# Cutting the weight loads differently: W1's chunk 13 together with chunk 12, W2's chunks 9 to 12 in two slices

## The chip, the cores and the metric

The kernel runs on one core of a Trainium2 chip. The metric is the device time of one execution in microseconds (us); of several runs the median is given. Lower is better.

## What is computed

Linear attention over 8 batches, 8 heads, 576 positions and 64 channels, and then a two-layer network over the 4608 resulting rows of 512 channels:

```python
q_s = exp(q - max(q, -1)); q_s = q_s / sum(q_s, -1)      # per row
k_s = exp(k - max(k, 2));  k_s = k_s / sum(k_s, 2)       # over the positions
kv  = einsum('bhsd,bhse->bhde', k_s, v)                  # 64 x 64 per head
x   = einsum('bhsd,bhde->bhse', q_s, kv)                 # then heads side by side: (4608, 512)
h   = x @ w_in                                           # (4608, 2048)
g   = where(h > 0, h, exp(min(h, 0)) - 1)                # ELU
out = g @ w_out                                          # (4608, 512)
```

All inputs and the output are float32. W1 is `w_in` (512 x 2048, 4 MB), W2 is `w_out` (2048 x 512, 4 MB).

## The kernel before, in words

**Work and its order.** The hidden width of 2048 is cut into 16 chunks of 128 (`NCH`). A step (j, s) is chunk s of batch j; there are eight batches of 512 rows and a ninth group that collects the 64 rows left over from each batch. In `program` (L1146) each step runs, in this order: `hidden` (L882, with its matmuls in `hidden_mm`, L912), four matmuls 128x512 that make 128 hidden channels of 512 rows from X and W1; ScalarE's exponential (L895, or the pair L892 and L893 for some steps) and GpSimd's subtraction of one (L896); VectorE's combination into the tile GT (L925); and, three steps later (`LAG`), `project` (L927 to L936), four matmuls that add GT times the chunk's 128 rows of W2 to four output banks. So on TensorE a group of L912 and a group of L933 take turns, and the first projection needs W2's chunk 0 three steps after the first hidden product. A hidden product of chunk n writes one of three PSUM banks, the one that chunk n - 3 used; it waits until L925 has read that one.

**Queues.** The program is written out by hand as text tables. `START` (L42 to L50) is the order of the work on batch 0 before the steps begin; `FIRST` (L51 to L68) says what each step of batch 0 does besides its own work: three strings, the first run after the hidden matmuls, the second after the projection, the third after L925. The words of a string are carried out by `do` (L1018). Most of them belong to the attention of the next batch: `qmax`, `qsub`, `qexp`, `qsum`, `qmul` the softmax of Q; `kturn`, `kacross`, `diag`, `kspread`, `copy`, `ksub`, `kexp` the one of K; `vconv`, `kv`, `kfac` the product with V; `pturn` and `pturn0` (L744, L766) transposes by TensorE of the softmax of Q; `att`, `xc` the rows of X. `load` issues a load on SyncE's queue (SP), `hold` makes SP wait for the latest hidden product before it issues more.

**The weights.** `w1:a:b` loads W1's chunks a to b - 1 (`load_w1`, L252, issue at L255) and `w2:a:b` W2's (`load_w2`, L259, issue at L262). Both are issued by GpSimd (POOL) between its other instructions, into a queue of its own (q0 in the profile; SP's loads of Q, K and V are q1). One load has one semaphore: whoever needs any chunk of a slice waits until the whole slice has landed. A slice of W1 is 128 partitions times four row pieces of 512 bytes per chunk; a slice of W2 is 128 partitions times one row of 2048 bytes per chunk. The order of W loads before is, in `START`: W1 1-3, W1 0, W2 0-1, W1 4-5, W2 2, W1 6-8, W2 3, W2 4-5; in `FIRST`: step 1 W1 13, then W1 9-11; step 2 W2 6-8; step 4 W1 12, then W2 9-12; step 5 W1 14-15; step 12 W2 15, then W2 13-14. After batch 0 all weights stay in SBUF.

Of the kernel before, what the change touches and what calls it, by code (L numbers as in the profile page):

```python
# [15 lines left out]
R = 4  # L16
# [33 lines left out]
         "pwide:B:act w2:3:4 att:2 att:3 xc:2 load:Q:1:A load:Q:1:R w2:4:6 h:0:2 xc:3 kmax2:AB ")  # L50
FIRST = {  # L51
    0: ("qmax:A ksub:R:dve", "", "qsub:0:dve"),
    1: ("w1:13:14", "w1:9:12", "qsub:1:dve"),
    2: ("", "qmax0:R", "w2:6:9"),
    3: ("hold qexp:A", "load:Q:1:B:act", ""),
    4: ("w1:12:13", "w2:9:13", "load:K:1:R qsum:A qsub0:R:dve"),
    5: ("w1:14:16", "kturn", "kacross vconv:R qmax:C"),
    6: ("", "qmul:A hold", "load:V:1:RAB"),
    7: ("qexp0:R", "", "diag qsub:2:dve"),
# [1148 lines left out]
```

## Time and profile before

| | |
|---|---|
| median of 3 runs | 309.68 us |
| lowest and highest | 309.59 and 310.59 us |
| span of the profiled execution, first to last instruction | 308.1 us |
| median less that span | 1.6 us |
| TensorE busy | 297.6 us (97%) |
| VectorE, ScalarE, GpSimd busy | 235.0, 192.9, 171.3 us |
| moved by DMA | 51.63 MB, of it 8.39 MB on q0 |

The profile is of one execution. PE is TensorE's matmuls, PEld its loads of stationary operands, which overlap the matmuls; DVE is VectorE, ACT ScalarE, POOL GpSimd, SP SyncE. A row of the timeline has the start in us from the span's start, the time in us, the engine, the line, the operation with output and input, how many there are, and in brackets the idle time before it with what ended it. In a row of waits stand the total in us, how many times, and the longest. In a row of DMA issues stand how many, the size, and the time from issue to landing.

### The profile page before, as it was taken

The page shows a single profiled execution, that of the slowest core. Times are in us where ns is not written, and L with a number is a line of the kernel's source. Part 1 is how long each engine was busy: PE and PEld are TensorE (multiplying, and loading weights), DVE is VectorE, ACT ScalarE, POOL GpSimd, SP SyncE. Part 2 cuts the span into 40 slices and gives each one's busy share as a digit, 9 for nine tenths or more (in the row PEclk, how much of TensorE's full clock was granted, in tenths as well). Part 3 has the DMA queues.
Part 4 walks back from the last instruction along what each step waited for, and adds up shares of the span by engine and source line. Part 5 has one row for each costly group of instructions (what it writes and reads, how often), then busy time and mean ns, then how long its engine had stood idle before and what let it go on. Part 6 is the DMA issues. An engine that isn't in the chain of part 4 may idle for free.

```text
span 308.1 us, 4839 instructions
## 1 busy us (share of the span) xinstructions
PE 297.6 (97%) x1733; PEld 240.1 (78%) x1733; DVE 235.0 (76%) x400; ACT 192.9 (63%) x358; POOL 171.3 (56%) x215
## 2 busy tenths in 40 slices
PE   7789899999999999999999999999999999999995
PEld 4467677788878888888888888888888888888884
DVE  6988978979959897999889988998895353335442
ACT  2678975577559784877587758775877543334432
POOL 2968873686436743786278637863686333333440
PEclk9999999999999999999999999999999999999999
DMA  7999999985708993768475846590512030003004
GB/s 261 393 340 364 372 345 257 273 253 145 191 3 246 261 251 105 223 122 231 133 217 144 208 143 209 146 198 3 172 23 57 2 136 0 0 2 136 0 0 136
DMA packets 60584, 51.63 MB, mean 168 GB/s; under 512 B 26897, under 2 KB 50705, under 8 KB 60561
## 3 DMA queue, kind: packets, MB, share of 16 engines
q1 hardware_dynamic: 52960, 41.23, 47.7%
q0 software_dynamic: 6400, 8.39, 10.5%
q10 hardware_dynamic: 1200, 1.72, 2.0%
q8 instruction: 13, 0.21, 0.3%
q14 instruction: 11, 0.08, 0.1%
HBM read 38.27 MB, written 9.45 MB: 155 GB/s over the span
## 4 chain that ended last, share of the span: by engine, by line
PE 85%; DMA 6%; POOL 4%; ACT 2%; DVE 2%; issue 1%
PE bank L933 40%; PE bank L912 40%; DMA W2S<-in_moe_w_out_dram 5%; PE bank L827 2%; POOL W1S L255 1%; PE bank L598 1%; DMA QR<-in_q_dram 1%; POOL QR L679 1%; POOL QS L708 1%; PE bank L805 1%; DVE KT L326 1%; DVE QF L672 0%; PE bank L560 0%; ACT ES L895 0%; ACT ES L893 0%
## 5 line engine op out<-in xcount | busy, mean ns | idle before, releaser
L933 PE MATMUL bank<-W2S,GT 128*128 128x512 f32 x572 | 153.4, 391 | 1.4 <-DMA W2S<-in_moe_w_out_dram 1.2
L896 POOL TENSOR_SCALAR ES<-ES 128x512 f32<-128x512 f32 (+1 forms) x130 | 85.8, 662 | 117.3 <-ACT ES L895 117.3
L912 PE MATMUL bank<-XT,W1S 128*128 128x512 f32 x512 | 138.4, 392 | 0.5 <-issue 0.3
L925 DVE SCALAR_TENSOR_TENSOR GT<-bank,ES 128x512 fp32r<-128x512 f32 (+1 forms) x130 | 87.9, 681 | 54.4 <-PE bank L912 40.6
L933 PEld LDWEIGHTS bank<-W2S,GT 128*128 128x128 f32 x572 | 106.3, 188 | 23.6 <-DMA W2S<-in_moe_w_out_dram 1.6
L895 ACT ACTIVATE ES<-bank 128x512 f32<-128x512 f32 (+1 forms) x130 | 76.0, 592 | 70.9 <-PE bank L912 70.7
L912 PEld LDWEIGHTS bank<-XT,W1S 128*128 128x128 f32 x512 | 94.1, 188 | 19.9 <-ACT XT L814 0.9
L679 POOL TENSOR_TENSOR QR<-QR,QM 128x512 f32<-128x512 f32 (+1 forms) x21 | 24.9, 1187 | 0.6 <-DVE QM L672 0.5
L684 ACT ACTIVATE QR<-QR 128x1024 f32<-128x1024 f32 (+3 forms) x19 | 19.0, 1006 | 3.1 <-DVE QR L679 3.1
L855 ACT ACTIVATE XT<-bank 128x320 fp32r<-128x320 f32 (+1 forms) x30 | 15.0, 501 | 9.4 <-PE bank L827 9.3
L689 DVE TENSOR_REDUCE QZ<-QR 128x16 f32<-128x1024 f32 (+1 forms) x14 | 18.8, 1343 | 0.6 <-ACT QR L684 0.6
L672 DVE TENSOR_REDUCE QM<-QR 128x16 f32<-128x1024 f32 (+1 forms) x14 | 18.8, 1342 | 0.0
L912 PE MATMUL bank<-XTR,W1S 128*128 128x512 f32 x64 | 16.6, 389 | 0.0
L438 DVE TENSOR_TENSOR KR<-KR,NB 128x512 f32<-128x512 f32 x16 | 14.6, 938 | 0.0
L623 ACT ACTIVATE MB<-bank,KZ 64x64 fp32r<-64x64 f32 x44 | 10.1, 302 | 7.0 <-DVE KZ L614 6.9
L387 DVE TRANSPOSE_TENSOR_REDUCE KM<-KR 128x32 f32<-128x1024 f32 x12 | 14.4, 1226 | 0.0
L857 POOL CAST QT<-QW 128x1024 fp32r<-128x1024 f16 x12 | 12.5, 1039 | 2.9 <-DMA QW<-QS 2.9
L912 PEld LDWEIGHTS bank<-XTR,W1S 128*128 128x128 f32 x64 | 12.0, 188 | 2.5
L892 ACT ACTIVATE ES<-bank 128x512 f32<-128x512 f32 x15 | 8.9, 594 | 7.9 <-PE bank L912 7.9
L827 PE MATMUL bank<-QT,MB 128*128 128x320 f32 (+1 forms) x48 | 12.5, 300 | 0.7 <-ACT XT L855 0.7
L708 POOL TENSOR_TENSOR QS<-QR,QI 128x1024 f16<-128x1024 f32 (+1 forms) x7 | 12.5, 1783 | 0.4 <-DVE QI L691 0.4
L484 ACT ACTIVATE EK<-KR 128x1024 bf16<-128x1024 f32 x12 | 12.6, 1050 | 0.0
(108 smaller groups left out, 262.8 us busy)
## 6 DMA issues: line engine op xcount, KB each, us to landing
out_dram<-OSB SPq DMA_DIRECT2D x30, 256.0 KB, 2.7
KR<-in_k_dram SPq DMA_DIRECT2D x6, 1024.0 KB, 7.7
VR<-in_v_dram SPq DMA_DIRECT2D x6, 1024.0 KB, 6.3
QR<-in_q_dram SPq DMA_DIRECT2D x5, 1024.0 KB, 8.0
KR<-in_k_dram SPq DMA_DIRECT2D x8, 288.0 KB, 6.1
VR<-in_v_dram SPq DMA_DIRECT2D x8, 288.0 KB, 6.6
W1S<-in_moe_w_in_dram POOLq DMA_DIRECT2D x3, 768.0 KB, 9.2
QR<-in_q_dram SPq DMA_DIRECT2D x4, 512.0 KB, 11.2
```

What stands on the lines that cost most here:

```text
L672: self.op("dve", lambda: v.tensor_reduce(m, QR, AX.X, ALU.max), self.qkeys(b, part), self.qstat("QM", b, part))
L679: self.op(en, lambda: e.tensor_tensor(QR, QR, m, ALU.subtract), keys + self.qstat("QM", b, part), self.qown(b, part))
L684: self.op("act", lambda: a.activation(QR, QR, AF.Exp), keys, self.qown(b, part))
L689: self.op("dve", lambda: v.tensor_reduce(z, QR, AX.X, ALU.add), self.qkeys(b, part), self.qstat("QZ", b, part))
L708: self.op(en, lambda: e.tensor_tensor(out, QR, z, ALU.mult), keys + self.qstat("QI", b, part), [f"QS{x}" for x in cells])
L827: last = pe.matmul(self.bank[bank][:, a - c0:b - c0], self.MB[f][:, :, :].rearrange("p u d -> p (u d)"), self.QT[:, f, a - f * S:b - f * S ...
L855: self.op("act", lambda: e.activation(out, src, AF.Copy), reads, writes)
L895: self.op("act", lambda: a.activation(ES[:, x], ps[:, x], AF.Exp), [f"bank{bank}"], keys + mark)
L896: self.op("gp", lambda: g.tensor_scalar(ES[:, x], ES[:, x], -1.0, 1.0, ALU.add, ALU.mult), keys, keys)
L912: return pe.matmul(ps, self.W1S[:, kc, c * 128:(c + 1) * 128], x[:, kc, 0:SM], start=(kc == 0), stop=(kc == 3))
L925: self.op("dve", lambda: v.scalar_tensor_tensor(out[:, x], *how), [f"bank{bank}"] + eks + (["FINE"] if n < FINE else []), keys)
L933: return pe.matmul(self.bank[OB[t]][:, :], self.GT[n % NG][:, t * 128:(t + 1) * 128], self.W2S[:, c, :], start=(c == 0), stop=(c == NCH - ...
```

## The change

Three words move. W1's chunk 13 no longer has a load of its own in step 1 but comes in one slice with chunk 12 in step 4, and W2's chunks 9 to 12, one slice of 1 MB in step 4, become two of 512 KB, issued one behind the other at the same place. The number of W loads stays 16. The order of instructions is the same on TensorE, VectorE, ScalarE and SP; on GpSimd only the issues named differ.

```diff
 FIRST = {
     0: ("qmax:A ksub:R:dve", "", "qsub:0:dve"),
-    1: ("w1:13:14", "w1:9:12", "qsub:1:dve"),
+    1: ("", "w1:9:12", "qsub:1:dve"),
     2: ("", "qmax0:R", "w2:6:9"),
     3: ("hold qexp:A", "load:Q:1:B:act", ""),
-    4: ("w1:12:13", "w2:9:13", "load:K:1:R qsum:A qsub0:R:dve"),
+    4: ("w1:12:14", "w2:9:11 w2:11:13", "load:K:1:R qsum:A qsub0:R:dve"),
     5: ("w1:14:16", "kturn", "kacross vconv:R qmax:C"),
```

## The prediction

> **What bounds the kernel now.** I read the page first, for the engine that fills the span and for the chain of work that ended last.
>
> ```profile
> span 308.1 us, 4839 instructions
> ...
> PE 297.6 (97%) x1733; PEld 240.1 (78%) x1733; DVE 235.0 (76%) x400; ACT 192.9 (63%) x358; POOL 171.3 (56%) x215
> ...
> PE 85%; DMA 6%; POOL 4%; ACT 2%; DVE 2%; issue 1%
> ```
>
> TensorE is busy for 97% of the span and is 85% of the chain. So work on other engines is free as long as TensorE does not wait for it, and every microsecond in which TensorE stands still is a microsecond of the result. The 6% of DMA in the chain is the thing to look at. The view of waits says how much of it is TensorE standing still, and the timeline of its weight loads says where.
>
> ```profile
> PEld bank L933 <- DMA W2S<-in_moe_w_out_dram: 1.6, 2, 1.1
> PE bank L933 <- DMA W2S<-in_moe_w_out_dram: 1.2, 2, 0.9
> ```
>
> ```profile
> 36.00 0.45 PEld L744 LDWEIGHTS bank<-ID,QS 128*128 128x128 f16 x8 [0.27 <-ACT NB L471]
> 37.57 0.76 PEld L933 LDWEIGHTS bank<-W2S,GT 128*128 128x128 f32 x4 [1.12 <-DMA W2S<-in_moe_w_out_dram]
> ...
> 40.52 0.20 PEld L766 LDWEIGHTS bank<-ID,QSR 64*64 64x64 f16 x8 [0.35 <-DVE GT L925]
> 40.76 0.76 PEld L912 LDWEIGHTS bank<-XT,W1S 128*128 128x128 f32 x4
> ...
> 44.08 0.45 PEld L744 LDWEIGHTS bank<-ID,QS 128*128 128x128 f16 x8 [0.27 <-issue]
> 44.98 0.76 PEld L933 LDWEIGHTS bank<-W2S,GT 128*128 128x128 f32 x4 [0.45 <-DMA W2S<-in_moe_w_out_dram]
> ```
>
> There are just two such waits (1.6 us in 2 times on the loads). Both stand in front of a projection (line 933) whose W2 chunk is not there yet: chunk 6 at 37.57 and chunk 9 at 44.98. Without the wait, how early could the loads begin? The pair at 40.52 shows it: the small transposes' loads end at 40.72 and the next 128x512 group loads at 40.76, 0.04 later. So chunk 6's projection could begin at 36.45 + 0.04 = 36.49 and gains at most 37.57 - 36.49 = 1.08; chunk 9's could begin at 44.53 + 0.04 = 44.57 and gains at most 0.41. Together 1.49 us is the whole prize.
>
> The next question is what the late slices stood behind. POOL issues all weight loads; the timeline gives the issues, the view of DMA issues the time of each to landing.
>
> ```profile
> 19.42 0.70 POOL L262 DMA_DIRECT2D W2S<-in_moe_w_out_dram  x1
> ...
> 24.21 1.52 POOL L255 DMA_DIRECT2D W1S<-in_moe_w_in_dram  x2
> 25.71 0.76 POOL L262 DMA_DIRECT2D W2S<-in_moe_w_out_dram  x1
> 26.66 0.61 POOL L896 TENSOR_SCALAR ES<-ES 128x512 f32<-128x512 f32 x1 [0.19 <-ACT ES L895]
> 27.23 0.80 POOL L255 DMA_DIRECT2D W1S<-in_moe_w_in_dram  x1
> 28.02 0.76 POOL L262 DMA_DIRECT2D W2S<-in_moe_w_out_dram  x1
> 29.37 0.61 POOL L896 TENSOR_SCALAR ES<-ES 128x512 f32<-128x512 f32 x1 [0.58 <-ACT ES L895]
> 29.93 0.78 POOL L255 DMA_DIRECT2D W1S<-in_moe_w_in_dram  x1
> 31.09 1.94 POOL L708 TENSOR_TENSOR QS<-QR,QI 128x1024 f16<-128x1024 f32 x1 [0.38 <-DVE QI L691]
> ```
>
> ```profile
> W2S<-in_moe_w_out_dram POOLq DMA_DIRECT2D x1, 512.0 KB, 10.7
> ...
> W1S<-in_moe_w_in_dram POOLq DMA_DIRECT2D x1, 256.0 KB, 7.9
> W1S<-in_moe_w_in_dram POOLq DMA_DIRECT2D x1, 768.0 KB, 9.1
> W2S<-in_moe_w_out_dram POOLq DMA_DIRECT2D x1, 768.0 KB, 11.8
> W1S<-in_moe_w_in_dram POOLq DMA_DIRECT2D x1, 256.0 KB, 13.4
> W2S<-in_moe_w_out_dram POOLq DMA_DIRECT2D x1, 1024.0 KB, 16.9
> W1S<-in_moe_w_in_dram POOLq DMA_DIRECT2D x1, 512.0 KB, 18.0
> ```
>
> Issue plus time to landing, in order: W2 4-5 at 19.42 + 10.7 = 30.1; W1 chunk 13 at 24.21 + 7.9 = 32.1; W1 9-11 at 24.97 + 9.1 = 34.1 (the second of the two issues that last 1.52); W2 6-8 at 25.71 + 11.8 = 37.5; W1 12 at 40.6; W2 9-12 at 44.9; W1 14-15 at 47.9. They land in the order of issue, 2.0, 2.0, 3.4, 3.1, 4.3 and 3.0 us apart, and long after their issue: this is one queue with a backlog, and W1 chunk 13 stands at its head although nothing needs it before 46.
>
> **The change part by part.** *W1 chunk 13 leaves the place ahead.* Two landings of the backlog, W1 9-11 and W2 6-8, now have 256 KB less before them. What that is worth is not in the trace as such, so I bound it by two rows of the queues.
>
> ```profile
> q0 software_dynamic: 979, 1.44, 140.1%
> q1 hardware_dynamic: 37, 0.03, 3.3%
> ```
>
> ```profile
> q0 software_dynamic: 308, 0.37, 64.1%
> q1 hardware_dynamic: 310, 0.32, 57.9%
> ```
>
> The first pair is the stretch 30 to 34 us: the weights' queue (q0) has the DMA engines to itself, 979 packets and 1.44 MB in 4 us, 0.36 MB/us. The second is 41 to 43 us, where SyncE's loads (q1) run beside it: nearly the same count of packets each, and q0 gets 0.19 MB/us. The least that 0.26 MB are worth is then 0.26/0.36 = 0.7 us; the most is the 2.0 us of the slot between the landings at 30.1 and 32.1. Below the least there would be only a queue that does not close up, and the even succession of landings excludes this. W2 6-8 thus lands between 35.5 and 36.8. I take 36.0, nearer to the full slot, since a slice that starts earlier also puts more of itself into the stretch where q0 is alone. Against the 36.49 at which TensorE wants it, the first wait is gone; at the low end 0.3 us of it stay. Gain 1.08.
>
> *W1 12 now comes with 13.* The 512 KB land when 12 and 13 both are there. All that was ahead of them plus themselves is the same set of bytes as was ahead of W1 12 before, so 40.6 is the late bound.
>
> ```profile
> 42.16 1.17 PE L933 MATMUL bank<-W2S,GT 128*128 128x512 f32 x4
> 43.16 1.08 PE L912 MATMUL bank<-XT,W1S 128*128 128x512 f32 x4
> ...
> 46.02 1.07 PE L912 MATMUL bank<-XT,W1S 128*128 128x512 f32 x4
> ...
> 49.03 1.09 PE L912 MATMUL bank<-XT,W1S 128*128 128x512 f32 x4
> ```
>
> The hidden product of chunk 12 ran at 43.16 and would want it at 43.16 - 1.08 = 42.08: 1.5 us to spare. Chunk 13 runs later still. Cost nothing; the cover is that slack.
>
> *W2 9-12 becomes 9-10 and 11-12.* Before, 1 MB took 4.3 us between landings; half of it, at the same pace, 2.2. So W2 9-10 lands near 40.6 + 2.2 = 42.8 at the latest, and TensorE wants it at 44.57 - 1.08 = 43.49. The second wait goes, +0.41. Unsplit, at 44.9 or a little before, it would have kept the wait and made it longer, since TensorE arrives earlier: the split is what lets the first gain through. W2 11-12 lands near 45.0 and is first used in the projection after 49: nothing.
>
> *W1 14-15 is late next.* It landed at 47.9 and was used at 49.03, 1.1 us of slack. TensorE now comes at 49.03 - 1.49 = 47.54. If the slice still lands at 47.93, 0.39 us are lost and the gain is 1.10. If it lands 0.4 earlier, the gain is 1.49. The merge takes 512 short packets (128 partitions times four row pieces of one chunk) out of q0, and where both queues move packet for packet each of them has let one of q1 go ahead. I take 0.3 us earlier, three quarters of the way, because the late slices all run in the shared stretch: gain 1.40.
>
> The Trainium skill, "DMA: Bandwidth & Descriptors", section "Queues, rings and completion order", says that each DMA engine goes round between the queues that have work, packet by packet; the counts at 41 to 43 us agree (308 and 310), those at 30 to 34 us (979 and 37) show it only where q1 had packets ready. By it the merged slice is ahead by its fewer packets (sum 1.49), by bytes alone it is not (sum 1.10).
>
> *POOL's own time.* One issue of 0.76 us goes from step 1, one comes in step 4, and SP's queue is passed by none of them. In step 4 POOL would reach the ES of line 896 at 28.02 + 2 x 0.76 = 29.54, where it ran at 29.37: 0.17 us late. Then the next issue and the multiplication of line 708 follow, and the latter already waits 0.38 us for VectorE. So it is hidden; without that cover, the 0.17 us would delay one GT that is needed only three steps later. No row of other engines moves.
>
> *What else must keep up when TensorE is 1.1 to 1.5 us earlier?*
>
> ```profile
> 41.87 0.68 DVE L925 SCALAR_TENSOR_TENSOR GT<-ES,bank 128x512 fp32r<-128x512 f32 x1
> 42.47 1.10 DVE L456 TENSOR_TENSOR KR<-KR,NB 128x576 f32<-128x576 f32 x1
> 43.49 0.67 DVE L925 SCALAR_TENSOR_TENSOR GT<-ES,bank 128x512 fp32r<-128x512 f32 x1
> 45.88 0.69 DVE L925 SCALAR_TENSOR_TENSOR GT<-bank,ES 128x512 fp32r<-128x512 f32 x1 [1.72 <-POOL ES L896]
> ```
>
> VectorE is full from 40 to 44.2 and does not follow TensorE there. The bank of hidden chunk 13 is freed by the GT that ends at 42.55; TensorE comes at 46.02 - 1.49 = 44.53. The bank of chunk 14 comes free at 44.16, wanted at 47.54. From 45.88 on VectorE waits for the chain that TensorE starts, and moves with it. So nothing else stops TensorE, and the rest of the span, where TensorE hardly waits, moves forward whole.
>
> **Sum.** 1.08 + 0.41 - 0.09 = 1.40 us of a span of 308.1. The median of the runs shown, 309.68, lies 1.6 above the span; that part is before the first and after the last instruction and does not change. Predicted: 309.68 - 1.40 = 308.3 us.
>
> **The rivals.**
>
> *Only part arrives.* For: the first slot is worth only its bytes (0.7 us, W2 6-8 at 36.8), and W1 14-15 lands no earlier, or somewhat later than 47.9 since two W2 slices lie before it. With W1 14-15 at 48.4, TensorE's hidden product of chunk 14 begins 0.6 earlier than before: 309.1 us. Against: the same bytes and fewer packets are ahead of it.
>
> *The wait only moves.* W1 14-15 lands at 49.0, and TensorE starts chunk 14 when it did: 309.7 us, no change. This would also be the picture if W2 6-8 did not come earlier at all, that is, if the change did not do what it says; the successive landings speak against it.
>
> *The split costs a slot.* If what a W2 slice takes in the shared stretch is not its bytes but its turn, each of the two takes the 4.3 us of the old one. With W1 12-13 earlier by the whole slot, at 38.6, W2 lands at 42.9 and 47.2 and W1 14-15, 3.0 later, at 50.2: chunk 14 begins 1.2 us later than 49.03, and the result is 310.9 us. It decides from the moment W1 14-15 lands after 49.03. For: the 256 KB slice of W1 12 took 3.1 us, not a quarter of 4.3, so short slices do pay more than bytes. Against: that slice had 512 packets like the 1 MB one, whereas half of W2's rows are half the packets. The Trainium skill, "DMA: Bandwidth & Descriptors", section "Bandwidth", asks to batch transfers to 1 MiB and more, and its section on the anatomy of one DMA puts the constant part at about 2.0 us each; by it alone the split would cost 2.0 us and the merge would give 2.0 us back before that. The landings 2.0 us apart for 768 KB (32.1 to 34.1) show that this constant part is not paid in series here.
>
> **How the numbers follow.** Forecast (both waits go, W1 14-15 nearly in time): 0.62, its own range 307.9 to 308.7, that is gains of 1.0 to 1.8. Part arrives: 0.20, about 309.1, of which a third is beyond 0.3%. The wait moves: 0.08. The slot: 0.10. The measurement tells apart about 0.3%, 0.93 us: faster means below 308.75. Faster 0.62 + 0.07 = 0.69; same 0.13 + 0.08 = 0.21; slower 0.10. The range 307.9 to 309.5 takes in the forecast and the partial case and leaves out the rest.
>
> **What the changed profile would show.** Right: no wait for W2S before line 933 in the view of waits; chunk 6's projection at about 36.5, chunk 9's at 43.5, chunk 14's hidden product at 47.5 to 47.9, all later rows of TensorE earlier by 1.1 to 1.5, span near 306.7. Wrong: a wait of line 912 or 933 for W1S or W2S between 42 and 52 us; W1 14-15 landing after 48; or, after 52 us, TensorE idle where it wasn't, which would mean that something I take as following TensorE is paced by a transfer.

## The result, and the profile after

| | before | changed |
|---|---|---|
| median of 9 runs each | 309.84 us | 309.20 us |
| lowest to highest | 309.37 to 310.59 | 308.78 to 309.42 |
| span of the profiled execution | 308.1 us | 307.4 us |

The ratio, which uses all runs and not the medians alone (they differ by 0.64 us), is 0.9975, with a 95% interval of 0.9964 to 0.9986: 0.8 us faster, with 0.4 to 1.1 in the interval. 1.4 us were forecast. The sign is right and the time lies in the stated range of 307.9 to 309.5; about half of the gain is missing. It lies outside the 307.9 to 308.7 of the forecast case itself, and above the 308.75 below which the prediction would call it faster: the outcome that it gave 0.69 did not come, the one that it gave 0.21 did.

I read the weight loads of TensorE in the profile after first, at the places that were shown of before.

```profile
36.73 0.45 PEld L744 LDWEIGHTS bank<-ID,QS 128*128 128x128 f16 x8 [0.27 <-ACT NB L471]
37.14 0.76 PEld L933 LDWEIGHTS bank<-W2S,GT 128*128 128x128 f32 x4
...
43.64 0.45 PEld L744 LDWEIGHTS bank<-ID,QS 128*128 128x128 f16 x8 [0.27 <-DVE GT L925]
44.05 0.77 PEld L933 LDWEIGHTS bank<-W2S,GT 128*128 128x128 f32 x4
...
48.17 0.76 PEld L912 LDWEIGHTS bank<-XT,W1S 128*128 128x128 f32 x4 [0.22 <-DMA W1S<-in_moe_w_in_dram]
```

Both waits for W2S are gone: each projection's loads follow the small transposes at once. A wait of 0.22 us has come up in front of hidden chunk 14, for W1 14-15, the slice that the prediction called late next. But chunk 6's projection begins at 37.2, not 36.5. The issues and their times to landing say that the weights are not to blame.

```profile
24.93 0.77 POOL L255 DMA_DIRECT2D W1S<-in_moe_w_in_dram  x1
25.70 0.75 POOL L262 DMA_DIRECT2D W2S<-in_moe_w_out_dram  x1
...
27.95 0.80 POOL L255 DMA_DIRECT2D W1S<-in_moe_w_in_dram  x1
28.75 1.42 POOL L262 DMA_DIRECT2D W2S<-in_moe_w_out_dram  x2
...
30.74 0.80 POOL L255 DMA_DIRECT2D W1S<-in_moe_w_in_dram  x1
```

```profile
W1S<-in_moe_w_in_dram POOLq DMA_DIRECT2D x1, 768.0 KB, 8.7
W2S<-in_moe_w_out_dram POOLq DMA_DIRECT2D x1, 768.0 KB, 10.2
...
W1S<-in_moe_w_in_dram POOLq DMA_DIRECT2D x1, 512.0 KB, 12.3
W2S<-in_moe_w_out_dram POOLq DMA_DIRECT2D x1, 512.0 KB, 13.6
...
W1S<-in_moe_w_in_dram POOLq DMA_DIRECT2D x1, 512.0 KB, 17.4
```

W2 6-8 landed at 25.70 + 10.2 = 35.9 (36.0 was forecast, 37.5 before), W1 12-13 at 40.3, W2 9-10 at 42.4 (42.8 forecast), W1 14-15 at 48.1 (47.6 forecast). What is late is TensorE itself, before any of the words changed can act. The timeline of TensorE shows the first hidden group, first before and then after:

```profile
18.93 0.69 PE L766 MATMUL bank<-ID,QS 64*64 64x64 f16 x32 [0.26 <-POOL QS L708]
19.88 1.17 PE L912 MATMUL bank<-XT,W1S 128*128 128x512 f32 x4 [0.26 <-issue]
```

```profile
19.65 0.69 PE L766 MATMUL bank<-ID,QS 64*64 64x64 f16 x32 [0.26 <-POOL QS L708]
20.59 1.16 PE L912 MATMUL bank<-XT,W1S 128*128 128x512 f32 x4 [0.25 <-issue]
```

It begins at 20.59 and not at 19.88, 0.71 us later. VectorE's timeline shows where the difference arises, at its second reduction over a slice of Q (line 672), before and then after:

```profile
7.45 0.69 DVE L672 TENSOR_REDUCE QF<-QR 128x8 f32<-128x512 f32 x1
```

```profile
8.16 0.69 DVE L672 TENSOR_REDUCE QF<-QR 128x8 f32<-128x512 f32 x1 [0.64 <-DMA QR<-in_q_dram]
```

In after it stood still for 0.64 us until that slice of Q had landed; in before it did not wait. From this row to the first hidden group it is 12.4 us in each of the ten profiles that have the same code up to there (12.41 to 12.43), and in nine of them the row waits for Q. So the start follows the landing of one of SP's first loads, by 9 us at the latest, while the words changed act only from 24 us on.

From the first hidden group to the end, before took 308.1 - 19.88 = 288.2 us and the changed kernel 307.4 - 20.59 = 286.8: the forecast 1.4 us are there, and 0.7 of them went to a later start. Why that holds for the medians too, and not for these two executions alone, is what the runs had to find out.

### The profile page after: what moved, and what is told of

Same layout as the page of the kernel before. It is cut to its first block, busy times and chain, and to the rows that moved or that the text cites. A ratio compares the mean times of both kernels' runs of the same rounds, so it can differ in the third digit from the quotient of the medians.

```text
span 307.4 us, 4838 instructions
## 1 busy us (share of the span) xinstructions
PE 298.6 (97%) x1733; PEld 240.5 (78%) x1733; DVE 234.8 (76%) x400; ACT 193.1 (63%) x358; POOL 171.8 (56%) x215
## 3 DMA queue, kind: packets, MB, share of 16 engines
q0 software_dynamic: 5888, 8.39, 10.1%
## 4 chain that ended last, share of the span: by engine, by line
PE 91%; POOL 3%; DVE 2%; DMA 2%; issue 1%; SPq 1%; ACT 0%
PE bank L933 43%; PE bank L912 42%; PE bank L827 2%; DMA QR<-in_q_dram 2%; PE bank L598 1%; POOL W1S L255 1%; DVE KT L326 1%; POOL QR L679 1%; PE bank L560 1%; SPq L277 1%; PE bank L805 1%; POOL W2S L262 0%; POOL VB L857 0%; DVE QM L672 0%; PE bank L1007 0%
```

## The experiments

Three theories stood at the outset. **A, cover:** the start differs from execution to execution, and in the kernel before the waits for the weights hide part of a late start; in the changed kernel nothing does. **B, draw:** all moves with the start, the true gain is 1.4 us. **C:** the change itself makes the start later.

| run | median us | median of before, same chip | ratio, 95% interval |
|---|---|---|---|
| e1_before_again | 310.11 | 310.35 | 0.9997 (0.9981 to 1.0013) |
| e2_after_again | 308.90 | 310.35 | 0.9956 (0.9939 to 0.9972) |
| e3_merge_alone | 309.34 | 310.35 | 0.9973 (0.9961 to 0.9986) |
| e4_split_alone | 309.38 | 310.35 | 0.9972 (0.9958 to 0.9986) |
| e5_before_late | 309.87 | 310.04 | 1.0003 (0.9992 to 1.0014) |
| e6_after_late | 310.13 | 310.04 | 1.0007 (0.9997 to 1.0016) |
| e7_order | 308.94 | 310.04 | 0.9967 (0.9956 to 0.9979) |
| e8_moved_alone | 309.45 | 310.04 | 0.9985 (0.9971 to 1.0000) |
| e9_before_mid | 309.75 | 310.15 | 0.9988 (0.9975 to 1.0001) |
| e10_after_mid | 309.47 | 310.15 | 0.9985 (0.9973 to 0.9997) |
| e11_after_third | 309.06 | 310.15 | 0.9965 (0.9951 to 0.9979) |
| e12_order_again | 308.89 | 310.15 | 0.9958 (0.9943 to 0.9972) |

### The same two kernels again

No edit in either.

> The kernel before, once more. After's profile began its first hidden group 0.71 us later than before's (20.59 against 19.88), before the change can act. Theory A (cover): the start differs from execution to execution; in the kernel before, a later start is partly hidden, because the landing of the weights and not the start sets when TensorE goes on: if this profile's first hidden group is at about 20.6, the two waits for W2S are shorter (0.8 instead of 1.5 us) and chunk 9's projection still begins near 45.0. Rival B (draw): weights land later with the start, waits stay 1.5 us, everything is 0.7 later, span about 308.8. Rival C (the change makes the start later): first hidden group at 19.9 again, waits as before. Time: equal to before under all three.

> The changed kernel, once more. A and B: the first hidden group can be anywhere from 19.9 to 20.6; where it is early, the span is near 306.7. C: again at 20.6 and span 307.4. Time: 0.6 to 0.8 us under before by A and C; by B 1.4 us, the nine runs so far being a poor draw.

The kernel before, in a second execution, began its first hidden group later too, and waited less. From TensorE's timeline and the view of waits of e1_before_again:

```profile
20.52 1.16 PE L912 MATMUL bank<-XT,W1S 128*128 128x512 f32 x4 [0.23 <-issue]
...
37.79 1.20 PE L933 MATMUL bank<-W2S,GT 128*128 128x512 f32 x4 [0.51 <-DMA W2S<-in_moe_w_out_dram]
```

```profile
PEld bank L933 <- DMA W2S<-in_moe_w_out_dram: 1.2, 2, 0.7
PE bank L933 <- DMA W2S<-in_moe_w_out_dram: 0.8, 2, 0.5
```

The start is 0.64 later than in before's first profile, chunk 6's projection only 0.22 later (37.57 to 37.79), and the span 0.3 longer (308.4). So 0.4 of 0.64 us were hidden: A's sign, though not the full 0.7 that it expected, since 1.2 us of the waits were left where it expected 0.8, and chunk 9's projection moved to 45.25. C falls: the kernel before starts at 20.5 as well. The changed kernel's second profile started at 20.36, waited for no weight at all and spanned 306.9. On this chip it was 1.4 us faster than before (0.9 to 1.9). That is the time that B expected and not the 0.6 to 0.8 of A, so this pair leaves the two open. At an equal start the profiles give 1.2 us: e7_order below, without a wait for a weight, also began at 20.52 and spanned 307.2 where the kernel before spanned 308.4. The start of 19.88, on which the prediction's sum was built, was the earliest in the ten profiles that have the same code ahead of the first hidden group.

### Each half of the change alone

```diff
     # e3_merge_alone, against before
-    1: ("w1:13:14", "w1:9:12", "qsub:1:dve"),
+    1: ("", "w1:9:12", "qsub:1:dve"),
-    4: ("w1:12:13", "w2:9:13", "load:K:1:R qsum:A qsub0:R:dve"),
+    4: ("w1:12:14", "w2:9:13", "load:K:1:R qsum:A qsub0:R:dve"),
     # e4_split_alone, against before
-    4: ("w1:12:13", "w2:9:13", "load:K:1:R qsum:A qsub0:R:dve"),
+    4: ("w1:12:13", "w2:9:11 w2:11:13", "load:K:1:R qsum:A qsub0:R:dve"),
```

> Only W1's part of the change: chunk 13 comes with chunk 12, W2 9 to 12 stay one slice. My reading: the first wait goes, the second grows, since TensorE arrives 1.1 earlier at chunk 9 while the 1 MB slice lands where after's second half landed (44.5 in its profile, which TensorE reached at 44.05): a wait of about 0.5 us there, nothing more at W1 14; span 0.2 to 0.5 above after's at the same start. Rival (the split brings nothing, the merge all): the 1 MB slice lands by 44.0 and there is no wait; same time as after.

> Only W2's part: 9 to 12 in two slices, W1 13 still alone ahead. My reading: the wait at chunk 6 stays (0.9 to 1.1 us at the start of before's profile, less at a later start); W2 9-10 lands about 2.2 us earlier than 44.9, so the wait at chunk 9 goes; gain against before 0.4 us at most. Rival (a further slice costs the queue a turn): W1 14-15 lands 1 to 3 us later than 47.9 and TensorE waits for it; slower than before by up to 2 us.

The merge alone missed its expectation: its profile, with the latest start of all (21.25), shows no wait for a weight. These are its issue of W2 9-12, the time to landing, and the loads at chunk 9:

```profile
29.39 0.75 POOL L262 DMA_DIRECT2D W2S<-in_moe_w_out_dram  x1
```

```profile
W2S<-in_moe_w_out_dram POOLq DMA_DIRECT2D x1, 1024.0 KB, 14.2
```

```profile
44.27 0.45 PEld L744 LDWEIGHTS bank<-ID,QS 128*128 128x128 f16 x8 [0.27 <-issue]
44.68 0.77 PEld L933 LDWEIGHTS bank<-W2S,GT 128*128 128x128 f32 x4
```

The 1 MB slice landed at 29.39 + 14.2 = 43.6, 1.1 us before it was wanted. With a start 0.7 to 0.9 us earlier, as in e2_after_again and after, little of that would be left by this estimate, so this profile cannot say what the split adds; the times leave 0.5 us to it (0.9973 against 0.9956) with intervals that overlap.

The split alone did as expected. Its weight loads, and its times to landing for W2 9-10 and W1 14-15:

```profile
37.85 0.76 PEld L933 LDWEIGHTS bank<-W2S,GT 128*128 128x128 f32 x4 [0.60 <-DMA W2S<-in_moe_w_out_dram]
...
44.37 0.45 PEld L744 LDWEIGHTS bank<-ID,QS 128*128 128x128 f16 x8 [0.27 <-DVE KR L456]
44.77 0.77 PEld L933 LDWEIGHTS bank<-W2S,GT 128*128 128x128 f32 x4
```

```profile
W2S<-in_moe_w_out_dram POOLq DMA_DIRECT2D x1, 512.0 KB, 14.3
...
W1S<-in_moe_w_in_dram POOLq DMA_DIRECT2D x1, 512.0 KB, 17.6
```

The wait at chunk 6 stays (0.60), the one at chunk 9 is gone: W2 9-10, issued at 28.83, landed at 43.1. W1 14-15, issued at 30.83, landed at 48.4, where e1_before_again, with the same start within 0.2 us, had it at 48.5. So the further slice cost the queue nothing that can be seen: the prediction's rival on the slower side, 310.9 us by two full turns, falls here. The Trainium skill, "DMA: Bandwidth & Descriptors", section "Bandwidth", asks for batches of 1 MiB and more; in a queue with a backlog this case's runs show no loss from half that size. That the split alone gave 0.9 us is more than the 0.4 expected at most, which lies at the lower edge of its interval (0.4 to 1.3).

### TensorE held back on purpose

```diff
     # e5_before_late against before, e6_after_late against the changed kernel; e9, e10: warm:4:3
-    "... kfac:B:act warm:1:3 att:1 att:0 ..."
+    "... kfac:B:act warm:7:3 att:1 att:0 ..."
```

> The kernel before with six more idle matmuls of line 1093 ahead of the first hidden group (they compute nothing that is used; a group of x4 takes 0.91 us, so about 1.4 us of TensorE). Theory A (cover): the weights keep their own pace, so a TensorE that comes later waits less for them: the waits for W2S fall from 1.2 to 1.6 us to about 0.5 or less, and of 1.4 us added only 0.5 to 0.9 arrive at the end. Rival B (all moves with the start): waits as before, the whole 1.4 us arrive, about 311.7.

> The changed kernel with the same six idle matmuls. A: it has no waits that could hide them, so the 1.4 us arrive whole (at most 0.2 less, for the wait at W1 14), about 310.4, and the gap to the kernel before with the same matmuls shrinks to between 0.2 and 0.7 us. B: the gap stays at 1.4 us.

This is the decisive pair. Six matmuls of no use ahead of the first hidden group cost the kernel before nothing (ratio 1.0003), and they cost the changed kernel 1.2 us: 310.13 against the 308.94 of e7_order on the same chip, which differs from the changed kernel only in the order of the last two slices. The gap between before and changed is gone. B, which expected the whole 1.4 us in both, falls. A has the sign right and the size wrong: it expected 0.5 to 0.9 us to arrive in the kernel before and a gap of 0.2 to 0.7 us to remain, but the runs show neither (by the interval of 1.0003, at most 0.4 us arrive). In the profile of e5_before_late the two waits are gone as well. TensorE's rows of the idle matmuls and of hidden chunk 4, first before and then e5_before_late:

```profile
17.71 0.50 PE L1093 MATMUL bank<-GT,ONES 128*128 128x512 f32 x1
...
25.50 1.07 PE L912 MATMUL bank<-XT,W1S 128*128 128x512 f32 x4
```

```profile
17.75 1.90 PE L1093 MATMUL bank<-GT,ONES 128*128 128x512 f32 x7
...
26.84 1.07 PE L912 MATMUL bank<-XT,W1S 128*128 128x512 f32 x4
```

And the loads at chunks 6 and 9 in e5_before_late:

```profile
37.33 0.45 PEld L744 LDWEIGHTS bank<-ID,QS 128*128 128x128 f16 x8 [0.27 <-ACT NB L471]
37.74 0.76 PEld L933 LDWEIGHTS bank<-W2S,GT 128*128 128x128 f32 x4
...
44.23 0.45 PEld L744 LDWEIGHTS bank<-ID,QS 128*128 128x128 f16 x8 [0.27 <-issue]
44.64 0.77 PEld L933 LDWEIGHTS bank<-W2S,GT 128*128 128x128 f32 x4
```

The six add 1.40 us to the one of before, as expected (the 0.91 us of the expectation is what four add to a running group; by themselves the four of e10_after_mid take 1.21). Hidden chunk 4 begins at 26.84, 1.34 us after its place in before (25.50), and chunk 9's projection at 44.6, 0.3 us before its place there. A later TensorE cannot make W2 land earlier by itself, and yet it did: W2 6-8 took 9.4 us from its issue at 26.81 and landed at 36.2, not 37.5. The timeline of SP has the reason. Its loads of V wait in `hold` for hidden chunk 6, and these rows are before and e5_before_late:

```profile
30.48 2.52 SPq L277 DMA_DIRECT2D VR<-in_v_dram  x4
```

```profile
31.82 2.40 SPq L277 DMA_DIRECT2D VR<-in_v_dram  x4
```

And the queues from 34 to 38 us, before and then e5_before_late:

```profile
q1 hardware_dynamic: 396, 0.83, 63.7%
q0 software_dynamic: 576, 0.64, 60.2%
```

```profile
q0 software_dynamic: 870, 1.01, 106.9%
q1 hardware_dynamic: 212, 0.45, 33.9%
```

The V loads come 1.34 us later, and in these 4 us the weights' queue moves 1.01 MB where it moved 0.64. W1 9-11, the slice ahead, had landed at the same time in both (34.1 and 34.2), so the difference arises after it. The trace also has the landing on each of the 16 DMA engines: 12 of them had their part of W2 6-8 by 34.6 in before and by 35.0 in e5_before_late, the last at 37.5 and 36.2. It is the few slowest engines that differ. So a late TensorE is hidden in two ways: it comes later to the wait, and the competing loads that follow it come later too. That W2 6-8 lands earlier for this reason rests on two profiles of each kind (36.2 and, with half the dose, 36.6, against 37.5 and 37.8 without); landings also differ by themselves, as the third run of the changed kernel shows below.

> The kernel before with three more idle matmuls of line 1093, half of the earlier dose, about 0.7 us of TensorE. Theory A (the waits for the weights cover a later start, microsecond for microsecond, until they are used up): the time is that of the kernel before within 0.3 us, as with six. Rival (the wait covers a fixed share only): 0.3 us or more above.

> The changed kernel with the same three. A: nothing covers them, 0.5 to 0.8 us above the changed kernel in this call, about 309.6, so that the gap to the kernel before with three is half the gap without, 0.3 to 0.7 us. Rival: the gap is unchanged, 0.8 to 1.4 us.

Half the dose agrees: nothing lost by the kernel before (0.9988; 1 lies just inside its interval), 0.6 us by the changed one (0.9985 against 0.9965 for e11_after_third on the same chip; 0.4 by the medians). The gap of the two is 0.1 us, below the 0.3 to 0.7 expected; the second way of hiding would account for it, but the intervals, 0.4 us to each side, leave room for the expected gap as well. Profiles of both show no wait for a weight.

### The order behind, and moved without merging

```diff
     # e7_order, e12_order_again, against the changed kernel
-    4: ("w1:12:14", "w2:9:11 w2:11:13", "load:K:1:R qsum:A qsub0:R:dve"),
-    5: ("w1:14:16", "kturn", "kacross vconv:R qmax:C"),
+    4: ("w1:12:14", "w2:9:11", "load:K:1:R qsum:A qsub0:R:dve"),
+    5: ("w1:14:16 w2:11:13", "kturn", "kacross vconv:R qmax:C"),
     # e8_moved_alone, against the changed kernel
-    4: ("w1:12:14", "w2:9:11 w2:11:13", "load:K:1:R qsum:A qsub0:R:dve"),
+    4: ("w1:12:13 w1:13:14", "w2:9:11 w2:11:13", "load:K:1:R qsum:A qsub0:R:dve"),
```

> The changed kernel with W2 11-12 issued behind W1 14-15. W1 14-15 then has 512 KB less ahead of it and lands 1 to 2 us earlier, W2 11-12 lands where W1 14-15 did, near 48, and is used near 50. If the 0.22 us wait at chunk 14 in the profile is the last of the weights' waits, there is none here, and the time is 0 to 0.2 us under the changed kernel's; if POOL's second issue ahead of the multiplication of line 708 matters, it is above.

> The order with W2 11-12 behind W1 14-15 once more, beside the changed kernel itself: within 0.2 us of it; below it by 0.1 to 0.2 if the wait of 0.22 us at chunk 14 is there in most executions, equal if it is rare.

> The changed kernel with W1 12 and 13 issued one behind the other and not as one slice: moved, not merged. If the place in the queue is what counts, chunk 6 and chunk 9 have no wait, and the time is the changed kernel's within 0.3 us. If the 512 short packets that the merge saves count, W1 14-15 lands about 0.5 us later against its issue than in the changed kernel and TensorE waits 0.3 to 0.7 us for it at an early start.

With the order turned, W1 14-15 landed 14.8 us after its issue at 30.59, at 45.4 instead of 48.1, and no profile of it shows a wait for a weight. The time is 308.94 and 308.89, 0.2 us under e11_after_third beside the second and within its interval: no loss, and no gain that can be told. The version with moved but not merged slices had a late start in its profile (21.06) and no wait; its ratio, 0.9985, is worse than e7_order's 0.9967, but the intervals overlap, so whether place or merging did it stays open in the times. In its profile W1 14-15, issued at 31.95, landed 15.0 us later and not 0.5 us later than the changed kernel's 17.4, but at another start.

### The changed kernel a third time

> The changed kernel a third time, beside the others on one chip: 0.8 to 1.4 us under before, spread of its runs half of before's, since its time follows the start alone. If 0.8 or less comes again, the starts on this chip are late ones.

The gain came as expected, 1.1 us (0.6 to 1.5), the halved spread did not (308.53 to 310.17 in 11 runs, before 309.31 to 310.94 in 28). Its profiled execution took 309.91 us and shows why. The view of waits:

```profile
PEld bank L912 <- DMA W1S<-in_moe_w_in_dram: 0.6, 2, 0.4
PEld bank L933 <- DMA W2S<-in_moe_w_out_dram: 0.4, 1, 0.4
```

It started at 20.42, like e2_after_again, but W2 6-8 took 11.9 us to land where it took 10.5 there. One DMA engine is the difference: 15 of the 16 had their part by 35.3 (35.4 in e2_after_again), the last at 37.4 (36.0). The landing differs from execution to execution too, by more than the 0.5 us to spare that the prediction left, and then the waits come back.

## Why the prediction was right, and where its size was off

**Both waits and what they hide: right.** Chunk 6's projection came 16.58 us after the first hidden group where it had come 17.69 after (1.11 less, 1.08 forecast); chunk 9's 23.48 where it had been 25.10, 1.62 less (1.49 forecast). Shown by the profiles, and by e4_split_alone for the second wait by itself.

**The landings: right** to about 0.5 us, and so was what is late next: W1 14-15, with a wait of 0.22 us where 0.09 was counted. By the prediction's own list this wait, and the landing at 48.1 where "after 48" was a sign of being wrong, speak against it; they cost 0.2 us. That W1 14-15 comes 0.3 us forward is not shown: from its issue it took 18.0 and 17.9 us in the two profiles of before and 17.6 with the split alone, but 17.4, 17.0 and 18.1 in the three of the changed kernel. The merge did take the 512 packets out of q0 (6400 before, 5888 after); what they are worth stays open.

**POOL's reordering and VectorE as cover: right.** Neither put a new wait on TensorE: from the first hidden group to the end the profile gained the forecast 1.4 us.

**The term that was mis-sized is the prize itself, "Together 1.49 us is the whole prize".** It is the prize of one execution, the one with the earliest start seen. At a start 0.64 us later the kernel before has only 1.2 us of waits on its loads; with TensorE held back by 1.3 us it has none and the change is worth nothing (1.0003 against 1.0007). The prediction set the time of one execution against the median with only the 1.6 us around the span between them, and took for granted that the start is the same in all. (In every run whose span is known, the time lies about 1.8 us above it; 1.6 came from setting the span of one execution against the median of others.) And it took the landings as the same in all, which e11_after_third does not bear out. From the first hidden group to the end the two profiles of before take 288.2 and 287.9 us; the six of the changed kernel and its variants that show no wait, or only the 0.22 of after, take 286.5 to 286.8, at starts from 20.36 to 21.25, and e11_after_third, with its waits, 287.7. So without the waits a later start arrives whole. Over the three comparisons the change is worth 0.8, 1.4 and 1.1 us.

**The rivals.** "Only part arrives" came nearest in time (309.1), but by another mechanism than the one it named: not the queue's slot but the start and the landings of the execution. That the measured time lies in the range is owed to this case having been taken in, and so in part to luck. "The wait only moves" is what e11_after_third's profile shows in part. "The split costs a slot" fell with e4_split_alone.

**Open:** why the slice of Q lands earlier in one execution than in another, why single DMA engines lag with W2 6-8, and what share of the hiding each of its two ways has.

## What to carry to other kernels

A wait for data that come at their own pace is slack for everything ahead of it: before its length is counted as gain, look at how much the arrival of the waiting engine differs between executions, because the wait covers that difference and its removal lays it bare. One profile gives one draw of both. Holding the engine back by a known amount, in both kernels, tells such a wait from one that moves with the start.

## What the runs showed of the hardware that was not expected

TensorE's first hidden group began anywhere from 19.88 to 21.25 us in ten profiles with the same code ahead of it, in nine of them 12.4 us after a wait for one slice of Q. A slice of W2 has landed when the slowest of the 16 DMA engines has its part: in before 13 of them had W2 6-8 by 35.1 and the last three between 36.7 and 37.5. And SP's V loads, issued at 30.48, moved next to nothing until 34 us (37 packets on q1 from 30 to 34) while the weights' queue had a backlog: the two queues did not share evenly from the issue on. Whether the backlog is the reason is not shown.
